# Transposing the softmax A by DMA from the fifth batch on, with a new start and new orders of work in a one-core attention and MLP kernel

## The chip, the cores and the metric

The kernel runs on one core of a Trainium2 chip. A core has TensorE (PE: matmuls and transposes, its weight loads are shown apart as PEld), VectorE (DVE), ScalarE (ACT), GpSimd (POOL), SyncE (SP, which here only issues DMAs) and 16 DMA engines that move data between the core's memory and HBM, or within the core's memory. The engines run beside each other and wait for each other through semaphores. The metric is the time of one execution in microseconds (us): 263.59 before, the median of 15 runs that lie between 263.0 and 264.41.

## The reference

The input is a batch of 8 with 8 heads, 576 tokens and a head size of 64. Attention in the manner of Nyström with 32 landmarks is followed by a two-layer MLP:

```python
q_lm = q.reshape(B, H, m, S // m, D).mean(axis=3)      # m = 32 landmarks of 18 tokens each
k_lm = k.reshape(B, H, m, S // m, D).mean(axis=3)
A  = softmax(scale * q    @ k_lm.T)                    # 576 x 32 for each head
Bm = softmax(scale * q_lm @ k_lm.T)                    # 32 x 32
C  = softmax(scale * q_lm @ k.T)                       # 32 x 576
Z  = Bm.T / (norm1(Bm) * norminf(Bm) + 1e-6)
for _ in range(6):
    Z = 2 * Z - Z @ Bm @ Z                             # Newton steps to the inverse of Bm
x = (A @ Z @ C @ v), heads side by side                # 4608 x 512
h = x @ w_in                                           # w_in 512 x 2048
out = (max(h, 0) ** 2) @ w_out                         # w_out 2048 x 512
```

## The kernel before

Work goes batch by batch. For each batch the attention part makes a transposed softmax A (tile `AT`, heads and landmarks on the partitions, tokens along the row) and a folded weight `G` = Z C v w_in. So the first layer is `h = G^T AT` (`mlp_in`, L822: four matmuls of 288 columns for each of 16 slices of the 2048 features), then ReLU on ACT (L826, tile `r`), the square on DVE (L827, tile `gT`), and the second layer (`mlp_out`, L851: 16 matmuls of 512 columns for each tile of 128 tokens, 36 such tiles in all), whose result is copied out by ACT and stored by ACT's DMA queue.

The attention part of batch b+1 is done while the MLP of batch b runs. Its steps have two-letter names. `pk`, `pq` copy k and q into the layout that is needed (`prepare`, L281), `mk`, `mq` make the segment means on PE with the 0/1 masks `seg` (L342), `tk`, `tq`, `tt` transpose k, q and the last 64 tokens, `lm` and `ls` make the landmark softmax, `ib`, `if`, `jo`, `jl`, `nu`, `nn` are the Newton steps, `sq`, `sk`, `tl` the scores of A and C with their exponentials, `as` the sums of A's rows, `ar` the scaled A (tile `an`, L584, written by DVE), `at` the transpose of `an` into `AT`, `cv` the product of C and v, `wt` and `gg` the folded weight `G`.

In `at` (`a_transposed`, L589 to L598) half a batch, five blocks of 128 tokens by 128, is turned by five PE transposes into PSUM (L596), and copied to `AT` by DVE or ACT (L685). The threshold `DMA_A` says from which batch on a transposing DMA on SP's queue does it instead; at 9 no batch does. The same exists for k and q (`DMA_T` = 3: from the fourth batch on the turning of k, q and their tails goes through SP's queue, L286 and L287).

The order on each of PE, DVE, ACT and SP is written out by hand. `HEAD` orders the first batch's attention (tokens such as `w:16`, 16 filler matmuls of 512 columns whose result nobody reads, or `w:1:256`, one of 256 columns). `PLANS` has one string for each batch: `h` is one slice of `mlp_in`, `s` its square, a bare number is so many matmuls of `mlp_out`, and a step's name does that step for the next batch (with `+` for the batch after). Each engine runs its instructions in the order in which these strings emit them. POOL's queue issues nearly all loads, which turn f32 into bf16 on the way, in one chain (from L132, `load`); `LOADS` is the order of the first of them.

Batch 0's start: SP loads the first k as f32 in one DMA of 1024 KB, and DVE and ACT turn its two halves into bf16 (`ck`, L717 and L718). POOL meanwhile issues the tails of k and q and q in two halves, makes the masks (`seg`, the identity, `mask4`), and then issues the rest of the loads.

Of the kernel before, what the change touches and what calls it, by code (L numbers as in the profile page):

```python
# [9 lines left out]
P = 128  # L10
# [4 lines left out]
BF16 = mybir.dt.bfloat16  # L15
F32 = mybir.dt.float32

B = 8
H = 8
S = 576  # L20
D = 64
M = 32
SEG = S // M
# [4 lines left out]
NC4 = 4  # L28
TAIL = S - NC4 * P
# [3 lines left out]
DMA_A = 9  # L33
# [3 lines left out]
    "w:16 ck tk1 mk w:1:256 w:1:256 ek1d w:1:256 w:1 tk0 tt w:1 w:1 cq0 cq1 ek0a mq tq0 tq1 "  # L37
    "lm w:1 et w:1:256 w:1 eq0a w:1:256 tl eq1d ls sum:0:4:5 w:1 ib w:1 w:1:256 sq1 w:1:256 "
    "if sk1 sum:1:2:5 w:1:256 w:1 sum:1:0:2 jo w:1:256 w:1:256 rec:1 w:1:256 row:1:0:3 "
    "row:1:3:5 w:1:256 sk0 w:1 sq0 jo w:1:256 w:1:256 w:1 w:1:256 sum:0:2:4 sum:0:0:2 w:1 jo "  # L40
    "rec:0 cv:0 cv:1 w:1:256 w:1:256 row:0:3:5 cr jo w:1:256 row:0:0:3 w:1:256 at:1 cba w:1 "
    "jl at:0 ea0d ea1a ct w:1:256 nu w:1:256 g:0 gl1d fv w:1 gf1d w:1 gf0a az gl0d"
)
LOADS = "w10 v0 w00 q1 w01 w11 o0 o1 o2 o3 v1"
PLANS = [
    (
        "pk h g:1 tt h pq h s tk1 s h s h tq1 s tk0 h h mk s s mq tq0 h lm s g:2 g:3 ls sk0 s h "
        "h ib 1 h 1 s if tl h jo 1 sq0 s 1 jo s s 1 h jo 1 sq1 1 jl h 1 nu h s s h nn 2 sk1 nu s "
        "1 s 8 as0 1 ar0 as1 2 ar1 5 nn1 cv 4 wt at0 2 gg0 2 at1 2 gg1 1"
    ),  # L50
    (
        "2 pk 1 h h 1 mk pq s mq 1 s h tq0 lm h ls h tt tq1 3 tl 1 s 1 h ib 1 s if s sq1 2 s h "
        "jo 1 as1 sq0 1 h h s 1 as0 tk1 1 jo 1 s 4 tk0 2 jo 1 h 1 s h 1 pk+ 1 jl ar1 h sk0 1 s 1 "
        "s nu h s 1 sk1 s h h nn s cv nu h 3 nn1 at1 s 3 s wt 3 ar0 2 gg0 3 at0 1 gg1 pq+"
    ),
    (
        "5 mk h 1 h mq s 2 h 5 lm s 2 ls 1 sk1 2 ib 3 h h s sk0 s if 1 s h 2 h 1 jo s h tl 3 jo "
        "1 s 2 h jo 1 s 2 h 3 s sq0 s 1 jl pk+ 4 sq1 2 as0 nu 3 h 1 nn 2 as1 1 pq+ 1 nu 1 h 1 "
        "ar1 h 1 s s h 1 nn1 cv 1 h 2 ar0 1 s wt h 1 at0 2 gg1 1 s at1 1 s 2 gg0 1 s"
    ),  # L60
    (
        "mk 2 h 1 mq 7 h 2 s lm s 1 ls 1 h sq1 1 h h 1 ib 1 s if sk1 1 s h s 2 h jo 1 s 1 h s 1 "
        "jo 2 h 1 pk+ jo 1 tl s h 2 jl as1 sq0 1 s h 1 s h nu s 1 h sk0 s 1 ar1 4 as0 nn 1 ar0 2 "
        "h 3 cv 2 s h nu 4 s nn1 1 at1 1 h wt 2 s 3 s gg1 1 at0 4 gg0 4 pq+"
    ),
    (
        "2 mk h 2 mq 4 h lm 1 h 1 s ls 1 sk0 s ib s 3 h h if 3 tl s 2 h h s 1 s jo 2 h h 1 jo s "
        "1 sq0 s 2 h 1 jo 5 s 10 jl pk+ s 3 sq1 h nu 1 h 1 h 3 as0 sk1 s 1 h 1 as1 ar1 5 s nn cv "
        "nu pq+ 4 s 2 nn1 ar0 h s 4 wt h 2 at0 s 1 gg0 2 s 1 at1 1 gg1 2"
    ),  # L70
    (
        "3 mk mq 3 h lm 3 h h ls 1 s 1 s ib 2 sq1 h 2 if 1 sq0 3 jo h 1 sk0 s jo 2 s h jo tl 4 "
        "as1 1 h 1 jl s sk1 h 3 pk+ s 4 nu h 1 s 2 s 1 s 4 as0 h 1 ar1 nn s 2 ar0 h cv h nu h s "
        "1 s 1 nn1 h 2 h pq+ s wt h 2 at1 2 gg0 at0 5 s 3 s s gg1"
    ),
    (
        "mk 1 mq 3 h s lm 1 h 3 ls 2 h s 1 ib 2 h 1 if sq1 s h 1 s 3 sq0 2 s h 2 s 2 jo h tl 3 "
        "jo 1 h h as0 jo 3 s h 1 s jl 1 s sk1 4 nu 2 as1 h nn 1 h 1 sk0 2 ar0 nu 1 s s 3 h h 1 "
        "cv 2 nn1 s h s 1 at0 1 wt h 2 s 1 ar1 gg0 1 at1 2 s 1 gg1 4 s"
    ),  # L80
    (
        "h 7 h 6 s 1 h 6 h 1 s 2 h s 2 h 6 s 13 h 2 s 2 h 1 s 1 s 5 s h 3 h 1 s s h 11 s 1 h s 8 "
        "h 1 h 1 h 1 s 4 s h 2 s s"
# [5 lines left out]
def kernel(  # L89
# [9 lines left out]
    nc = tc.nc  # L99
# [30 lines left out]
    behind, gate = [], []  # L130

    def load(dst, src, queue=nc.gpsimd):  # L132
        with tc.issue_after(behind[0].ins) if behind else nullcontext():
            d = queue.dma_start(dst, src)  # L134
        if gate:
            tc.add_manual_dep(
                d.ins, gate.pop().ins.name,
                mybir.DependencyInfo(mybir.DependencyClass.Sync, mybir.DependencyReason.DATA),
                reason="q first")
        if queue is nc.gpsimd:  # L140
            behind[:] = [d]
        return d

    def k_row(b):
        return TAIL if b % 2 == 0 else 0

    def q_row(b):
        return TAIL - k_row(b)
# [4 lines left out]
    def staged(b, nm):  # L153
        if (b, nm) == (0, "k"):
            t = stage[:, 0:2 * SIZE].bitcast(F32)
        else:
            o = SIZE * (1 + 2 * b + (nm == "q"))
            t = stage[:, o:o + SIZE]
        return t.rearrange("p (h c d) -> p h c d", h=H, c=NC4)

    def load_qk(b: int, X: dict):

        X["qkt"] = loads.tile([P, H, D], BF16, tag="qkt", name="qkt")

        def tails():
            for src, r0 in ((k, k_row(b)), (q, q_row(b))):
                load(X["qkt"][r0:r0 + TAIL, :, :],
                     src[b, :, NC4 * P:S, :].rearrange("h p d -> p h d"))

        if b > 0:  # L170
            tails()
        for nm, src in (("k", k), ("q", q)):
            if b < 3:
                X[nm + "raw"] = staged(b, nm)
            else:
                X[nm + "raw"] = loads.tile([P, H, NC4, D], BF16, tag="raw", name="raw")
            parts = ((0, H // 2), (H // 2, H)) if b == 0 and nm == "q" else ((0, H),)
            for lo, hi in parts:
                one = load(
                    X[nm + "raw"][:, lo:hi, :, :],  # L180
                    src[b, lo:hi, 0:NC4 * P, :].rearrange("h (p c) d -> p h c d", c=NC4),
                    nc.sync if b == 0 and nm == "k" else nc.gpsimd)
                if b > 0 and nm + "turn" in loaded[b - 1]:
                    tc.add_manual_dep(
                        one.ins, loaded[b - 1][nm + "turn"].ins.name,
                        mybir.DependencyInfo(mybir.DependencyClass.Sync,
                                             mybir.DependencyReason.DATA),
                        reason="behind the turning of the batch before")
            if b == 0 and nm == "k":
                tails()  # L190
# [12 lines left out]
    load_qk(0, loaded[0])  # L203

    def band(t, pattern, base, mult):
        return nc.gpsimd.affine_select(out=t, in_=t, pattern=pattern, compare_op=ALU.is_ge,
                                       fill=0.0, base=base, channel_multiplier=mult)
# [4 lines left out]
    band(seg[:, 0:NC4, :], [[1, NC4], [-SEG, M]], 0, NC4)  # L212
    band(seg[:, 0:NC4, :], [[-1, NC4], [SEG, M]], SEG - 1, -NC4)
    for s, t0 in ((NC4, NC4 * P), (NC4 + 1, NC4 * P - TAIL)):
        band(seg[:, s, :], [[-SEG, M]], t0, 1)
        band(seg[:, s, :], [[SEG, M]], SEG - 1 - t0, -1)
    ident_bf = const.tile([P, P], BF16, name="ident_bf")
    make_identity(nc, ident_bf[:])
    mask4 = const.tile([P, 4], F32, name="mask4")
    nc.vector.memset(mask4[:], 1.0)  # L220
    band(mask4[:], [[-32, 4]], 0, 1)
    masked = band(mask4[:], [[32, 4]], 31, -1)
    blk = const.tile([P, 4, M], F32, name="blk")
    nc.vector.tensor_copy(blk[:], mask4[:, :].unsqueeze(2).to_broadcast([P, 4, M]))
    blk_bf = const.tile([P, 4, M], BF16, name="blk_bf")
    nc.vector.tensor_copy(blk_bf[:], blk[:])
# [11 lines left out]
    nc.vector.tensor_copy(seg[:, NC4 + 2, :], seg[:, NC4, :])  # L238

    def load_rest(after):  # L240

        def w_in(i, j):
            load(
                w_in_bf[64 * i:64 * i + 64, :, 1024 * j:1024 * j + 1024],
                moe_w_in[256 * i:256 * i + 256, 1024 * j:1024 * j + 1024].rearrange(
                    "(j d) f -> d j f", d=D),
            )

        def w_out(j):
            load(  # L250
                w_out_bf[:, 4 * j:4 * j + 4, :],
                moe_w_out[512 * j:512 * j + 512, :].rearrange("(ft fp) c -> fp ft c", fp=P),
            )

        behind[:] = [masked]
        for x in LOADS.split():
            i = int(x[1])
            if x[0] == "w":
                w_in(i, int(x[2]))
            elif x[0] == "o":  # L260
                w_out(i)
            else:
                (load_v if x[0] == "v" else load_qk)(i, loaded[i])

# [33 lines left out]
    def attention(b: int, R: dict):  # L298
# [410 lines left out]
        def head_step(token):  # L709
# [5 lines left out]
            if name == "ck":  # L715
                raw = natural(0, "k")
                dve(X["k"][:, 0:2], raw[:, 0:2])  # L717
                load_rest(act(X["k"][:, 2:4], raw[:, 2:4]))  # L718
                st["qraw"] = natural(0, "q")
                X["tT"] = attn.tile([P, NPAIR, P], BF16, tag="tT", name="tT")  # L720
            elif name[:2] == "cq":
                lo = slice(4 * i, 4 * i + 4)
                dve(X["q"][:, :, lo, :], st["qraw"][:, :, lo, :])
# [250 lines left out]
```

The softmax here doesn't subtract the row's maximum and nothing guards it: scores larger than these inputs give would overflow.

## Time and profile before

| what | value |
|---|---|
| median of 15 runs | 263.59 us (263.0 to 264.41) |
| the profiled execution: time, span | 263.49 us, 261.8 us |
| PE busy | 251.5 us, 96% of the span |
| DVE, ACT, POOL busy | 176.5, 158.3, 45.2 us |
| the first `h` starts | 23.5 us |
| PE transposes of A (L596) | 80, in 16 sets of five |
| copies of AT from PSUM (L685) | 7 on DVE, 449 ns each; 7 on ACT, 640 ns each |
| transposing DMAs on SP's queue | 10 of k and q (T), 5 of the tails (tT) |
| first k on SP's queue | 1024 KB, landed 5.9 us after issue |

The profile is of one execution. Its span is what the engines show; the execution's time is 1.7 us longer. Busy time of PE is generous, since matmuls are pipelined and overlap. A row of a timeline has the start, the duration, the engine, the line, the operation, what it writes and reads, how often, and in brackets the idle time of the engine before it with what ended that. A row of the chain has the start, the duration and what the end was waiting for at that time.

### The profile page before, as it was taken

The page shows a single profiled execution, that of the slowest core. Times are in us where ns is not written, and L with a number is a line of the kernel's source. Part 1 is how long each engine was busy: PE and PEld are TensorE (multiplying, and loading weights), DVE is VectorE, ACT ScalarE, POOL GpSimd, SP SyncE. Part 2 cuts the span into 40 slices and gives each one's busy share as a digit, 9 for nine tenths or more (in the row PEclk, how much of TensorE's full clock was granted, in tenths as well). Part 3 has the DMA queues.
Part 4 walks back from the last instruction along what each step waited for, and adds up shares of the span by engine and source line. Part 5 has one row for each costly group of instructions (what it writes and reads, how often), then busy time and mean ns, then how long its engine had stood idle before and what let it go on. Part 6 is the DMA issues. An engine that isn't in the chain of part 4 may idle for free.

```text
span 261.8 us, 6949 instructions
## 1 busy us (share of the span) xinstructions
PE 251.5 (96%) x2850; PEld 154.1 (59%) x2894; DVE 176.5 (67%) x488; ACT 158.3 (60%) x278; POOL 45.2 (17%) x70
## 2 busy tenths in 40 slices
PE   7898999999999999999999999999999999999994
PEld 2674765476746655666556565666566655555453
DVE  5798777789985888699757588689776793232000
ACT  1556985478755857687557556775777764364210
POOL 8944234110010502501005010600000000000000
PEclk9999999999999999999999999999999999999999
DMA  8999999999539899995858989799501112112122
GB/s 183 200 194 206 206 206 189 210 212 88 115 41 210 128 168 224 149 171 116 136 107 97 198 162 180 107 198 202 108 16 40 43 43 80 40 43 81 40 80 80
DMA packets 69791, 34.65 MB, mean 132 GB/s; under 512 B 37376, under 2 KB 64256, under 8 KB 69760
## 3 DMA queue, kind: packets, MB, share of 16 engines
q0 software_dynamic: 39808, 17.83, 56.4%
q1 hardware_dynamic: 24704, 7.08, 16.1%
q10 hardware_dynamic: 5248, 9.31, 11.0%
q8 instruction: 22, 0.36, 0.6%
q14 instruction: 9, 0.07, 0.1%
HBM read 36.70 MB, written 9.44 MB: 176 GB/s over the span
## 4 chain that ended last, share of the span: by engine, by line
PE 89%; DVE 4%; DMA 2%; issue 2%; ACT 2%
PE ops L851 24%; PE h L822 24%; PE n L851 21%; PE n L530 3%; PE g L805 3%; DMA stage<-in_k_dram 2%; PE n L414 2%; PE n L342 2%; PE n L596 2%; PE idle L295 1%; PE n L614 1%; PE n L313 1%; DVE gT L827 1%; PE n L629 1%; DVE G L703 1%
## 5 line engine op out<-in xcount | busy, mean ns | idle before, releaser
L826 ACT ACTIVATE r<-h 128x576 bf16<-128x576 f32 x128 | 81.3, 652 | 45.5 <-PE h L822 33.7
L851 PE MATMUL ops<-w_out_bf,gT 128*128 128x512 bf16 (+1 forms) x300 | 76.8, 368 | 0.9 <-issue 0.3
L851 PEld LDWEIGHTS <-gT 128*128 128x128 bf16 x592 | 53.2, 98 | 38.7 <-issue 4.2
L827 DVE TENSOR_TENSOR gT<-r 128x576 bf16<-128x576 bf16 x128 | 54.9, 448 | 27.1 <-ACT r L826 27.0
L822 PE MATMUL h<-AT,G 128*128 128x288 bf16 x448 | 71.0, 286 | 0.2
L851 PE MATMUL n<-w_out_bf,gT 128*128 128x512 bf16 x252 | 69.7, 379 | 1.1 <-issue 0.3
L822 PEld LDWEIGHTS <-G 128*128 128x128 bf16 x512 | 47.7, 97 | 24.2 <-ACT AZ L795 0.7
L703 DVE CAST G<-g 128x1024 bf16<-128x1024 f32 x14 | 17.1, 1224 | 5.4 <-PE g L805 5.4
L862 ACT COPY o_sb<-ops 128x512 f32<-128x512 f32 (+1 forms) x19 | 10.9, 574 | 14.5 <-PE ops L851 14.5
L862 ACT COPY o_sb<-n 128x512 f32<-128x512 f32 x17 | 10.0, 587 | 12.9 <-PE n L851 12.8
L703 ACT CAST G<-g 128x1024 bf16<-128x1024 f32 x14 | 14.2, 1014 | 4.5 <-PE g L805 4.5
L295 PE MATMUL idle<-bd 128*128 128x512 bf16 (+1 forms) x47 | 12.3, 384 | 1.6 <-DVE bd L117 1.5
L530 PEld LDWEIGHTS <-T 128*128 128x128 bf16 x256 | 11.3, 98 | 4.2 <-issue 0.6
L134 POOL DMA_DIRECT2D raw<-in_k_dram x5 | 4.5, 890 | 53.0 <-DVE WT L698 15.5
L572 DVE TENSOR_REDUCE ra<-EA 128x20 f32<-128x640 f32 (+3 forms) x19 | 13.2, 703 | 0.3 <-ACT EA L560 0.3
L584 DVE TENSOR_TENSOR an<-EA,rra 128x640 bf16<-128x640 f32 (+2 forms) x18 | 13.2, 736 | 0.2
L530 PE MATMUL n<-bd,T 128*128 128x64 bf16 x256 | 12.7, 193 | 0.3 <-issue 0.2
L535 ACT ACTIVATE EA<-n 128x512 f32<-128x512 f32 x16 | 9.6, 598 | 3.3 <-PE n L530 3.2
L535 ACT ACTIVATE EC<-n 128x512 bf16<-128x512 f32 x16 | 9.5, 596 | 3.0 <-PE n L530 1.6
L134 POOL DMA_DIRECT2D raw<-in_q_dram x5 | 4.4, 885 | 37.2 <-DVE rc L445 17.1
L822 PE MATMUL h<-AZ,G 128*128 128x288 bf16 x64 | 10.0, 286 | 0.6 <-DVE AZ L795 0.4
L414 PEld LDWEIGHTS <-ED 128*128 128x128 bf16 x72 | 6.8, 98 | 6.1 <-DVE EY L453 0.5
(144 smaller groups left out, 286.9 us busy)
## 6 DMA issues: line engine op xcount, KB each, us to landing
out_dram<-o_sb ACTq DMA_DIRECT2D x31, 256.0 KB, 2.9
vm<-in_v_dram POOLq DMA_DIRECT2D x8, 512.0 KB, 10.7
raw<-in_k_dram POOLq DMA_DIRECT2D x5, 512.0 KB, 6.4
raw<-in_q_dram POOLq DMA_DIRECT2D x5, 512.0 KB, 6.1
w_in_bf<-in_moe_w_in_dram POOLq DMA_DIRECT2D x4, 512.0 KB, 11.9
w_out_bf<-in_moe_w_out_dram POOLq DMA_DIRECT2D x4, 512.0 KB, 16.8
out_dram<-o_sb ACTq DMA_DIRECT2D x9, 128.0 KB, 2.4
stage<-in_k_dram SPq DMA_DIRECT2D x1, 1024.0 KB, 5.9
```

The costliest lines, as they stand in the source:

```text
L295: nc.tensor.matmul(idle[:, 0:width], lhsT=z[:, 0:P], rhs=z[:, 0:width], start=True, stop=True)
L414: nc.tensor.matmul(res[a:a + w, qd, :], lhsT=diagonal[a:a + w, qd, :], rhs=moving(qd)[a:a + w], start=True, stop=True)
L530: nc.tensor.matmul(sc[:, c, j, :, :], lhsT=X[nm + "T"][:, c, p, :], rhs=BD[:, 1 if nm == "q" else 0, p, 0:64], start=True, stop=True)
L535: nc.scalar.activation(dst, sc.rearrange("p c j i m -> p c (j i m)"), AF.Exp, scale=SCALE)
L572: nc.vector.reduce_sum(ra[:, quads, lo:hi, :], EA[:, quads, lo:hi, :].rearrange("p q c (h m) -> p q c h m", m=M), axis=AX.X)
L584: on.tensor_tensor(an[:, i, lo:hi, :].rearrange("p c (h m) -> p c h m", m=M), EA[:, i, lo:hi, :].rearrange("p c (h m) -> p c h m", m=M), r ...
L703: (act, dve)[n % 2](G[:, :, n * 512:n * 512 + 512], gg[:])
L822: nc.tensor.matmul(h[:, j, 0:HALF], lhsT=G[:, qd, f * P:(f + 1) * P], rhs=AT[:, qd, a0 + j * HALF:a0 + (j + 1) * HALF], start=(qd == 0), s ...
L826: nc.scalar.activation(r.rearrange("p (j t) -> p j t", j=2), h[:, :, 0:HALF], AF.Relu)
L827: return lambda: nc.vector.tensor_tensor(gT[:, f, o:o + S], r[:], r[:], ALU.mult)
L851: nc.tensor.matmul(ops, lhsT=gT[:, f, t * P:t * P + P], rhs=w_out_bf[:, f, i * n:i * n + n], start=(f == 0), stop=(f == NF - 1))
L862: nc.scalar.copy(o_h, ops)
```

## The change

Three things change together. `DMA_A` goes from 9 to 4, so that for the fifth to the eighth batch (4 to 7) the two halves of `an` are each turned by one transposing DMA on SP's queue, without PE, PSUM and the copies. The first k is loaded in two halves by heads: the first four heads as f32 on SP's queue, the others as bf16 at the head of POOL's queue; the tails, the identity and q follow it there, and the other masks are made only after the first load of v has been issued. The copies that spread the masks on DVE become a step `sm` of `HEAD`. And `HEAD`, `LOADS` and all of `PLANS` are written anew: the fillers go from 51 to 21, batch 0's plan has 12 matmuls of the second layer where it had 36, the loads of w_in and v are in another order.

```diff
-DMA_A = 9
+DMA_A = 4
 HEAD = (
-    "w:16 ck tk1 mk w:1:256 w:1:256 ek1d w:1:256 w:1 tk0 tt w:1 w:1 cq0 cq1 ek0a mq tq0 tq1 "
...
+    "w:8 ck ch1 tk1 tk0 ek0a w:1 ek1d w:1:256 cq0 w:1 mk cq1 w:1 sm tt mq et tq0 eq0a tq1 lm "
...
-LOADS = "w10 v0 w00 q1 w01 w11 o0 o1 o2 o3 v1"
+LOADS = "v0 w10 w00 q1 w11 w01 o0 o1 v1 o2 o3"
 PLANS = [
     (
...
+        "pk h tt h g:1 s pq s tk1 h h tk0 tq1 h mk s s mq h s tq0 lm h h ls ib if sk0 s g:2 s jo "
+        "g:3 tl h jo 2 sq0 s jo h s 1 as0 jl sq1 h h 1 ar0 nu sk1 s s h nn 1 h as1 1 s nu cv nn1 "
+        "h s h wt 2 ar1 at0 gg1 s 1 s s 1 at1 2 gg0"
...
+        "3 mk mq 6 lm 1 ls 2 ib 1 h s h sq0 2 h 3 if sq1 h 1 s s 2 jo h s pk+ 2 sk1 jo 1 h s 1 h "
+        "s tl jo 4 s h 1 as0 h 1 ar0 4 jl 1 s sk0 h 1 h nu as1 s 4 h 2 s nn 2 at0 s 1 h nu ar1 3 "
+        "s h cv nn1 s h s 1 at1 h 2 wt 1 s s 1 pq+ 3 gg0 7 gg1 3"
...
+        "mk h 1 s 7 mq h 1 h lm 2 h 1 sk1 4 s 2 ls ib if 3 s tl 1 s h 1 jo s h 1 s 1 sk0 jo 1 h "
+        "1 cv h s 2 h 2 jo 1 sq0 1 h 2 as0 2 s 1 jl h s s h 1 ar0 s nu 4 sq1 h h 1 as1 4 nn 1 "
+        "ar1 3 s nu 3 h 1 nn1 s 5 s s wt h 4 gg1 at1 s 5 gg0 at0 2"
...
+        "6 h 1 s 6 h 1 h s s 5 h 3 h 1 h s s 1 h s 2 h 4 s 3 h 2 h 1 s 1 s 3 h 2 h s 1 h 1 s 1 s "
...
+    klo = stage[:, 0:SIZE].bitcast(F32).rearrange("p (h c d) -> p h c d", h=H // 2, c=NC4)
...
+    def load_first(X):
+        X["qkt"] = loads.tile([P, H, D], BF16, tag="qkt", name="qkt")
+        X["kraw"], X["qraw"] = staged(0, "k"), staged(0, "q")
+        load(klo, tokens_of(k, 0, 0, H // 2), nc.sync)
+        load(X["kraw"][:, H // 2:H, :, :], tokens_of(k, 0, H // 2, H))
+        for src, r0 in ((k, k_row(0)), (q, q_row(0))):
+            load(X["qkt"][r0:r0 + TAIL, :, :],
+                 src[0, :, NC4 * P:S, :].rearrange("h p d -> p h d"))
+        with tc.issue_after(behind[0].ins):
+            make_identity(nc, ident_bf[:])
+        for lo, hi in ((0, H // 2), (H // 2, H)):
+            load(X["qraw"][:, lo:hi, :, :], tokens_of(q, 0, lo, hi))
...
+    def masks():
+        with tc.issue_after(behind[0].ins):
+            band(seg[:, 0:NC4, :], [[1, NC4], [-SEG, M]], 0, NC4)
...
+            behind[:] = [band(mask4[:], [[32, 4]], 31, -1)]
+
+    def spread_masks():
+        nc.vector.tensor_copy(blk[:], mask4[:, :].unsqueeze(2).to_broadcast([P, 4, M]))
+        nc.vector.tensor_copy(blk_bf[:], blk[:])
+        nc.vector.tensor_copy(seg[:, NC4 + 2, :], seg[:, NC4, :])
...
-                raw = natural(0, "k")
-                dve(X["k"][:, 0:2], raw[:, 0:2])
-                load_rest(act(X["k"][:, 2:4], raw[:, 2:4]))
-                st["qraw"] = natural(0, "q")
+                kraw = natural(0, "k")
+                first_k = klo.rearrange("p h c d -> p c h d")
+                dve(X["k"][:, 0:2, 0:H // 2], first_k[:, 0:2])
+                act(X["k"][:, 2:4, 0:H // 2], first_k[:, 2:4])
+                load_rest()
+                st["kraw"], st["qraw"] = kraw, natural(0, "q")
...
+            elif name == "sm":
+                spread_masks()
+            elif name[:2] in ("ch", "cq"):
+                nm = "k" if name[1] == "h" else "q"
                 lo = slice(4 * i, 4 * i + 4)
-                dve(X["q"][:, :, lo, :], st["qraw"][:, :, lo, :])
+                dve(X[nm][:, :, lo, :], st[nm + "raw"][:, :, lo, :])
```

In the new order SP's queue has, for each of the batches 4 to 7, the two DMAs of A in one run, before, between or behind the transposing DMAs of the next batch's k and q.

## The prediction

> **What bounds the kernel now.** I read the page's busy times first, then the chain that ended last, then a table of stretches cut at the first `h` of each batch, then the chain and the timelines inside the stretches that the change touches. From the page:
>
> ```profile
> PE 251.5 (96%) x2850; PEld 154.1 (59%) x2894; DVE 176.5 (67%) x488; ACT 158.3 (60%) x278; POOL 45.2 (17%) x70
> PE 89%; DVE 4%; DMA 2%; issue 2%; ACT 2%
> ```
>
> PE is the bound, and nine tenths of the chain are matmuls. But this is an average. The stretches (us, busy time and instructions of PE, PEld, DVE, ACT, POOL, clock, DMA share, GB/s):
>
> ```profile
> 0.00:24.00 24.00, 20.88 (x320) 12.94 (x324) 17.84 (x59) 10.73 (x21) 16.33 (x33) 1.00 1.26 194
> 24.00:52.50 28.50, 27.45 (x404) 16.97 (x408) 22.11 (x56) 20.69 (x37) 8.51 (x11) 1.00 1.38 203
> 52.50:78.80 26.30, 25.93 (x349) 17.67 (x353) 23.59 (x65) 19.05 (x33) 2.27 (x3) 1.00 0.93 114
> 190.00:216.00 26.00, 25.46 (x283) 15.68 (x286) 19.41 (x57) 17.86 (x32) 0.00 (x0) 1.00 0.10 32
> ```
>
> From 52.5 us on PE is idle for 0.3 to 0.5 us in a stretch of 26: there a matmul taken away is time taken away. The head (0 to 23.5, where the first `h` starts) is different: PE's figure is padded with the fillers of L295 (3.8 us of the chain), and what runs is a chain of latencies. Its beginning, from the chain in order of time:
>
> ```profile
> 0.81 5.91 DMA stage<-in_k_dram
> 6.74 1.05 ACT nat L718
> 7.84 0.62 PE tps L313 x8
> 8.46 0.51 PE n L342 x20
> ...
> 9.32 0.69 DVE T L729
> 10.01 0.93 DVE nat L723 x2
> ...
> 10.99 0.41 PE n L342 x10
> ```
>
> Two arrivals carry it: k (landed at 6.72) and q's second half, whose DVE copy cannot end before about 10.9. After that DVE has hardly a gap: 5.5 us busy of the 6 from 14 to 20.
>
> **The change, part by part.** The profiled execution took 263.49 us (span 261.8 and 1.7 around it); the median is 263.59, so the sum made from the one holds for the other within 0.1. Less than 0.2% (0.53 us) either way cannot be told from no change.
>
> *The transposes of A leave PE.* Batches 4 to 7 lose two sets of five transposes each: 8 sets. What a set holds on PE is read from when the next matmul starts:
>
> ```profile
> 210.76 0.44 PE L596 MATMUL n<-ident_bf,an 128*128 128x128 bf16 x5
> 211.04 0.38 PE L851 MATMUL n<-w_out_bf,gT 128*128 128x512 bf16 x1
> ...
> 213.39 0.45 PE L596 MATMUL n<-ident_bf,an 128*128 128x128 bf16 x5
> 213.68 0.81 PE L851 MATMUL n<-w_out_bf,gT 128*128 128x512 bf16 x3
> ```
>
> 0.28 us, not the 0.44 in which the pipelined five overlap their neighbours: 8 x 0.28 = 2.2 us (bounds 2.1, from L596's 1.6% of the chain over 16 sets, and 3.5, from 0.44). These stretches have no idle PE to swallow it, so I take 2.2. Four copies of AT on ACT (0.64 each) and four on DVE (0.45) go too; ACT and DVE are idle a quarter of these stretches, so I count 0. If that cover were gone, 4.4 us of engine time would show.
>
> *Eight transposing DMAs on SP's queue, and a wait on PE.* The first `h` of batches 4 to 7 now waits for both. Behind it on PE stands everything, so a late landing is paid in full. The DMA was not run on `an` before. The nearest rows are the same instruction on four blocks (`tT`) and on sixteen (`T`); A has five. Issue to landing, tT and then T:
>
> ```profile
> DMA to landing us min/median/max: 4.3/4.8/6.0
> DMA to landing us min/median/max: 4.4/5.8/8.1
> ```
>
> SP held each tT for 1.3 us, so the pair is landed 1.3 + 4.8 = 6.1 us after the first can issue (bounds 5.5 and 9.6; I take 6.1, since five blocks are nearest to four). The least room is batch 7's. From `ar1` to its first `h` the new order has 29 steps of the output product (0.216 each, from 16 in 3.45 us), two `h` (0.49) and two `gg` (0.56): 8.4 us, 8.7 with the small products. `ar1` takes 0.8 on DVE and may stand behind two squares (0.8): 7.1 us remain, 1.0 to spare. Batch 6 waits after its `ar1` for one DMA (4.8) and has 7.3; batches 4 and 5 have 10 or more. Cost 0; at the upper bound 2.5 us in batch 7. On SP nothing urgent stands behind these DMAs: the T transposes of the next batch follow or go ahead, needed a plan later. DVE's next `ar` waits until the DMA has read `an` (one buffer), some 15 us later: hidden.
>
> A page of the Trainium skill speaks against this: "VectorE: DVE Perf Modes", The three transpose paths, gives 1309 ns for a 128x128 block by DMA against 390 by TensorE. By it a pair of ten blocks would take an estimated 13 us, 6 us more than batch 7 has. The trace's T rows (sixteen blocks inside 8.1 us at worst) disagree, and the sum goes by them.
>
> *k in two halves.* SP's f32 half and POOL's bf16 half go side by side; the 64-KB tails, which shared the queues with k, now follow it. Bytes read from HBM stay, so I bound k's landing by 6.7 (no gain) and 5.3 (both halves at the 383 GB/s that the DMAs reached from 4 to 5 us) and take 5.7. But this is hidden, for the masks move: POOL now issues five DMAs of the first batch's k and q, makes the identity, and issues v's two DMAs before it makes `seg`. From 1.31: 0.81 + 0.70 + 0.70 + 0.35 + 1.54 + 0.97 + 0.69 = 7.1, and the selects (1.3 to 1.6) end at 8.4 to 8.7, against 5.8. So `mk` cannot start before 8.4; it started at 8.30. What gains is q: less stands ahead of it, and its first half is copied before, not behind, T's copy. q's second half landed at about 10.0; now between 9.3 and 10.0, I take 9.5, copied by 10.1, `mq` done at 10.4. Three mask copies (1.3 us before, when POOL was busy; 0.5 to 1.3) now stand on DVE ahead of the copy into `bd`, so that starts near 11.0 instead of 11.44. The landmark exponential then stands on ACT behind T's copy (1.01): 11.85 against 12.43. That is 0.6; the shuffled DVE work behind it (8 us in both) I give another 0.2. Head: -0.8 us, bounds 0 (q no sooner, copies at their full 1.3) and -2.0 (k's whole 1.0 and the 1.0 us in which DVE idles).
>
> *Fewer fillers.* 16 warm-up matmuls become 8, and 35 later ones 13. They end at 4.9 instead of 7.2, and PE then idles until k is there. From the weight loads of the warm-up:
>
> ```profile
> 5.34 0.15 PEld L295 LDWEIGHTS <-bd 128*128 128x128 bf16 x1 [0.28 <-issue]
> 5.73 0.96 PEld L295 LDWEIGHTS <-bd 128*128 128x128 bf16 x5 [0.24 <-issue]
> ```
>
> Until 5.7 one came every 0.43 us, afterwards every 0.2: PE doubled its rate 4.2 us after its first matmul, though the granted clock reads 1.00 throughout. The new order gives it 3.4 us of work before a gap. I take 0, since about 2 us later PE is busy again and the head is held by DVE; upper bound +4.3: some 2.3 us of the head's 7 us of PE work at double length on the chain, and 2 us for the first 4 us of dense `h` at half rate.
>
> "TensorE: Matmul & The Clock Gate", Part 1, states a window of 3.4 us of sustained work, free-running, before full rate. Eight matmuls just fill it, but with the wrong phase the head would start slow. By the page as by the row the price is the 4.3 of the last sentences.
>
> *Orders.* From the first `h` to the last matmul, 23.5 to 258.1, the sum of PE's steady rates is about 230 us of 234.6, so 4.8 are stalls, 3.3 of them before 52.5. The new order does 12 output steps in batch 0's plan instead of 36, and loads v of batch 1 before the last two quarters of w_out. DVE needs 22.1 us there whatever the order, PE then 19.6: the stall stays about 3. I count 0, bounds +2.5 and -2.3.
>
> **Sum:** 263.5 - 2.2 - 0.8 = 260.5.
>
> **Rivals.**
> - *The new orders also close stalls.* For it: 35 fillers became 13, so PE is meant to wait less; 4.8 us of stalls are there. Against: DVE's load in the head and in batch 0's plan. Head -1.5, stalls -2.3: 257.5. Chance 0.18.
> - *PE stays at half rate through the head* (the other side). One mechanism: the gap from 4.9 to about 6.3. For it: full rate came 0.8 us after the new warm-up will have ended. Against: fillers are still strewn in. It decides if PE is slow beyond about 12.5, where half rate falls on the landmark chain; at the bound 260.5 + 4.3 = 264.8, slower. Chance 0.13.
> - *A's transposes land late.* 260.5 + 2.5 (batch 7) + 0.5 (another) = 263.5: no change. For it: 1.0 us of spare; against: the DMAs are idle by then (share 0.10 from 190 to 216). Chance 0.09.
> - *Batch 0's plan is held by DVE*, and the 2.5 us saved elsewhere stall there: 263.0, on the edge of faster. Chance 0.12.
>
> The forecast has 0.48. Faster: 0.48 + 0.18 + half of the last rival = 0.72; same: its other half and 0.04 of the late transposes = 0.10; slower: 0.13 and their other 0.05 = 0.18. The range leaves out the ends of the first two rivals: 257.5 to 264.2; the forecast's own is 259.3 to 261.7.
>
> **What would show it.** L596 x40 instead of x80, eight DMA_TRANSPOSE AT<-an landing in 4.3 to 6 us, and no PE idle time named to them at the first `h` of batches 4 to 7. First `h` at 22.7. `mk` at 8.4 or later, held by POOL's selects, with k landed before 6. Fillers and transposes after 6 us at 0.11 us each, if the rate is halved. Stretches of batches 4 to 6 shorter by 0.56 us each for the same work. I am wrong if the first `h` comes later than 23.5, or if PE idles over 1 us ahead of an `h` of batch 4 to 7.

## The result and the profile after

The changed kernel takes 267.82 us (median of 9 runs, 267.01 to 268.73), against 263.59 before (47 runs); the ratio is 1.0156, 95% interval 1.0144 to 1.0169. Forecast were 260.5 us and a range up to 264.2. The profiled execution took 267.15 us (span 265.0), 6.65 more than the forecast. From its page, busy times and the shares of the chain:

```profile
PE 248.5 (94%) x2781; PEld 151.8 (57%) x2824; DVE 175.5 (66%) x484; ACT 156.5 (59%) x275; POOL 46.1 (17%) x71
PE 78%; DMA 10%; POOL 4%; DVE 3%; issue 2%; ACT 1%; SPq 0%; POOLq 0%; ACTq 0%; DVEq 0%
```

PE has 3.0 us less to do (251.5 before), but the chain has DMA at 10% where it had 2%. The stretches, cut at the first `h` of batches 0 and 1 and at round times behind (same columns as before), show where:

```profile
0.00:23.46 23.46, 17.92 (x287) 11.44 (x290) 16.62 (x58) 10.22 (x21) 16.45 (x33) 1.00 1.24 176
23.46:48.00 24.54, 23.25 (x384) 15.44 (x389) 22.30 (x57) 20.38 (x38) 9.33 (x12) 1.00 1.35 202
...
133.00:162.00 29.00, 25.02 (x218) 14.61 (x221) 16.52 (x46) 14.67 (x28) 1.37 (x2) 0.94 0.80 132
162.00:190.00 28.00, 27.63 (x352) 17.14 (x355) 21.59 (x61) 18.84 (x34) 4.89 (x6) 1.00 1.15 158
190.00:216.00 26.00, 25.63 (x316) 15.75 (x310) 18.07 (x54) 16.57 (x30) 0.00 (x0) 1.00 0.27 69
```

In one stretch alone between the head and the end, 133 to 162, PE lacks 4.0 us, and its clock is 0.94 there and 1.00 in the others. The timelines of POOL, of SP's queue and of PE at that place:

```profile
125.53 0.89 POOL L134 DMA_DIRECT2D raw<-in_k_dram  x1 [15.33 <-DVE ED L409]
126.40 0.90 POOL L134 DMA_DIRECT2D raw<-in_q_dram  x1
127.27 0.91 POOL L134 DMA_DIRECT2D vm<-in_v_dram  x1
128.14 0.72 POOL L134 DMA_DIRECT2D vt<-in_v_dram  x1
```

```profile
128.56 3.98 SPq L595 DMA_TRANSPOSE AT<-an  x2
```

```profile
137.53 0.81 PE L860 MATMUL ops<-w_out_bf,gT 128*128 128x512 bf16 x3
138.66 0.41 PE L831 MATMUL h<-AT,G 128*128 128x288 bf16 x2 [0.33 <-DMA AT<-an]
142.33 0.40 PE L831 MATMUL h<-AT,G 128*128 128x288 bf16 x2 [3.26 <-DMA AT<-an]
```

Four loads (1.6 MB in bf16, cast from f32) were issued in the 3 us before the transposes of batch 4's A. The first half of `AT` is there some 10 us after its issue, at 138.6; the second after 12.4, at 142.29. PE stands for 3.6 us (0.33 and 3.26) at the first `h`. The DMAs of the loads, issue to landing, in the same stretch:

```profile
raw<-in_k_dram POOLq DMA_DIRECT2D x1, 512.0 KB, 6.1
raw<-in_q_dram POOLq DMA_DIRECT2D x1, 512.0 KB, 11.2
vm<-in_v_dram POOLq DMA_DIRECT2D x1, 512.0 KB, 15.1
...
vt<-in_v_dram POOLq DMA_DIRECT2D x1, 64.0 KB, 14.4
```

k and q of this bunch land at 131.6 and 137.6, v and its tail at 142.4 and 142.5: the first transpose was done behind k and q, the second only as the loads ran out. It is not the transposes alone: a store of 256 KB, issued by ACT's queue at the same time, took 8.4 us to landing, where the median of all of them is 2.6. Over all eight DMAs of A the landing is

```profile
DMA to landing us min/median/max: 2.6/3.9/12.4
```

and those of batches 5 to 7, with none of POOL's loads beside them, took 2.6 to 4.4. And PE does not go on at its old pace. Stretches of 2 us behind the wait:

```profile
142.00:144.00 2.00, 1.45 (x11) 1.11 (x12) 0.46 (x1) 1.19 (x3) 0.00 (x0) 0.76 0.64 40
144.00:146.00 2.00, 2.00 (x11) 1.10 (x11) 0.46 (x1) 1.17 (x3) 0.00 (x0) 0.50 0.04 8
146.00:148.00 2.00, 2.00 (x18) 1.24 (x16) 0.00 (x0) 1.46 (x3) 0.00 (x0) 0.89 0.35 131
148.00:150.00 2.00, 2.00 (x15) 1.08 (x13) 0.75 (x4) 0.29 (x1) 0.00 (x0) 1.00 0.00 0
```

The granted clock falls to half behind the 3.26 us without work. From the second half of the first `h` (142.33) to the fifth `h` PE takes 6.69 us:

```profile
149.02 0.65 PE L831 MATMUL h<-AT,G 128*128 128x288 bf16 x4
```

The same work takes 5.17 us at a clock of 1.00 (in the run with fillers below), so the half rate costs 1.5 us; the clock columns would give (0.24 + 0.50 + 0.11) x 2 = 1.7. So this place costs 3.6 + 1.5 = 5.1 us. The expectations below were written with 2.2 for the half rate, 5.8 in all; that was too much. Of the 6.65 missing, 0.8 more is the head: the first `h` starts at 23.46, not at 22.7.

Why the loads came in a bunch is read from the two orders. POOL may load raw k and q of batch 6 only when the copies and transposes of batch 5's have let go of the two buffers. Before, the copy of q (`pq+`) stood almost last in batch 3's plan (token 98 of 98), k's load went out at 122.21 and q's, v's at 140.15 to 141.9. From POOL's timeline before:

```profile
122.21 0.89 POOL L134 DMA_DIRECT2D raw<-in_k_dram  x1 [13.18 <-DVE gT L827]
140.15 0.88 POOL L134 DMA_DIRECT2D raw<-in_q_dram  x1 [17.05 <-DVE rc L445]
```

In the new plan `pq+` and `pk+` are tokens 26 and 34 of 97. The last of their transposes on SP's queue was issued at 119.23 and landed 5.7 us later, at 124.9, and at 125.53 POOL issued k, q and v in one run, 3 us ahead of A.

### The profile page after: what moved, and what is told of

Its sections match the earlier page's. It is cut to its first block, busy times and chain, and to the rows that moved or that the text cites. A ratio compares the mean times of both kernels' runs of the same rounds, so it can differ in the third digit from the quotient of the medians.

```text
span 265.0 us, 6831 instructions
## 1 busy us (share of the span) xinstructions
PE 248.5 (94%) x2781; PEld 151.8 (57%) x2824; DVE 175.5 (66%) x484; ACT 156.5 (59%) x275; POOL 46.1 (17%) x71
## 3 DMA queue, kind: packets, MB, share of 16 engines
q10 hardware_dynamic: 5248, 9.31, 10.1%
## 4 chain that ended last, share of the span: by engine, by line
PE 78%; DMA 10%; POOL 4%; DVE 3%; issue 2%; ACT 1%; SPq 0%; POOLq 0%; ACTq 0%; DVEq 0%
PE h L831 23%; PE ops L860 22%; PE n L860 20%; DMA stage<-in_q_dram 6%; DMA AT<-an 5%; PE n L534 3%; PE g L814 2%; PE n L346 2%; PE n L418 1%; POOL stage L134 1%; PE n L618 1%; POOL qkt L134 1%; PE n L633 1%; PE n L317 1%; DVE gT L836 1%
## 5 line engine op out<-in xcount | busy, mean ns | idle before, releaser
L860 PE MATMUL ops<-w_out_bf,gT 128*128 128x512 bf16 (+1 forms) x300 | 77.9, 368 | 0.9 <-DVE gT L836 0.2
L831 PE MATMUL h<-AT,G 128*128 128x288 bf16 x448 | 72.6, 288 | 3.8 <-DMA AT<-an 3.6
L860 PE MATMUL n<-w_out_bf,gT 128*128 128x512 bf16 x252 | 67.8, 381 | 1.3 <-issue 0.6
L576 DVE TENSOR_REDUCE ra<-EA 128x20 f32<-128x640 f32 (+3 forms) x19 | 13.3, 699 | 0.6 <-ACT EA L539 0.6
L346 PEld LDWEIGHTS <-nat 128*128 128x128 bf16 x256 | 8.5, 98 | 2.6 <-issue 0.8
L134 POOL DMA_DIRECT2D qkt<-in_k_dram x8 | 5.6, 701 | 24.4 <-PE n L356 15.1
L317 PEld LDWEIGHTS <-nat 128*128 128x128 bf16 x96 | 6.9, 110 | 4.9 <-DVE nat L732 2.5
```

The source lines that it names most:

```text
L346: nc.tensor.matmul(means[:, ti, p, :], lhsT=src.rearrange("p h d -> p (h d)"), rhs=seg[:, c + (ti if c == NC4 else 0), :], start=(n == 0 a ...
L576: nc.vector.reduce_sum(ra[:, quads, lo:hi, :], EA[:, quads, lo:hi, :].rearrange("p q c (h m) -> p q c h m", m=M), axis=AX.X)
L831: nc.tensor.matmul(h[:, j, 0:HALF], lhsT=G[:, qd, f * P:(f + 1) * P], rhs=AT[:, qd, a0 + j * HALF:a0 + (j + 1) * HALF], start=(qd == 0), s ...
L860: nc.tensor.matmul(ops, lhsT=gT[:, f, t * P:t * P + P], rhs=w_out_bf[:, f, i * n:i * n + n], start=(f == 0), stop=(f == NF - 1))
```

## The experiments

Two theories for the loss at this place. *Loads*: a transposing DMA is fast alone and slow when casting loads stand ahead of it in the DMA engines. *Transposes*: the five-block DMA, or two in a row on one queue, is that slow at this place whatever else runs.

**Five batches on PE.** Only batches 5 to 7 go by DMA.

```diff
-DMA_A = 4
+DMA_A = 5
```

> The changed kernel with DMA_A = 5: batch 4 turns A by PE again, batches 5 to 7 by DMA. Theory 'loads': the changed kernel loses its time at one place, where the second DMA of batch 4's A, issued at 129.9 us behind four loads of POOL (125.5 to 128.9), landed 12.4 us later. PE stood for 0.3 + 3.3 us and then ran about 4.5 us at half rate (granted clock 0.76, 0.50, 0.89), which is 2.2 more. Then this kernel saves 3.6 + 2.2 and pays two sets of transposes, 0.56: 267.8 - 5.8 + 0.6 = 262.6, and the granted clock is 1.000 again. Rival 'orders': the new orders lose all over the run and the wait is only where it shows: 266 or more.

Measured: 262.21 us (261.84 to 262.3), ratio 0.995 (0.9934 to 0.9967), 5.6 us below the changed kernel although PE has ten transposes more. No PE wait for `AT`; landings 2.6, 3.7 and 4.5 us (least, median, most). The loss is batch 4's alone.

**The load behind the transposes** (the ordered kernel, below). All of the change, but the load of k of batch b+2 is ordered behind the transposing DMA of batch b's A (and with it all that stands behind k on POOL's queue).

```diff
             one = load(X[nm + "raw"][:], tokens_of(src, b))
+            if nm == "k" and b >= 2 and "aturn" in loaded[b - 2]:
+                tc.add_manual_dep(one.ins, loaded[b - 2]["aturn"].ins.name, ...)
...
-                nc.sync.dma_start_transpose(AT[:, i, :]...
+                X["aturn"] = nc.sync.dma_start_transpose(AT[:, i, :]...
```

> The changed kernel, with all eight DMAs of A, but the load of k (and, as POOL issues in order, of q and v behind it) of the batch after next waits until A is turned. Theory 'loads': the transposing DMA is slow only because the loads stand in the same DMA rings ahead of it. Then batch 4's two DMAs land within 3 to 5 us, PE does not wait, and the loads, some 8 us later, are still in time: 267.8 - 5.8 = 262.0. Rival 'transposes': turning 10 blocks takes 10 us and more of itself, or two such DMAs hold each other up; then it still lands about 10 us after issue and the time stays at 267 to 268.

Measured: 261.8 us (261.44 to 262.19), ratio 0.9938 (0.9923 to 0.9953). POOL's timeline and the landings of A:

```profile
134.52 0.89 POOL L134 DMA_DIRECT2D raw<-in_k_dram  x1 [24.59 <-DMA AT<-an]
```

```profile
DMA to landing us min/median/max: 2.6/4.1/5.2
```

The same DMAs at the same time (128.29) land in at most 5.2 us when the loads go out at 134.52, 9 us later, PE does not wait for them, and the time falls by 6.0. This is the cause of the loss, shown by one rule of order. (In the two profiled executions the difference is 5.7: the 5.1 of this place and 0.5 by which the first `h` came earlier, at 22.93.) Whether it is the casting or only the bytes of the loads that hold the transposes up, no run separates.

**The old kernel with A by DMA.** Before, and `DMA_A` = 4 alone.

```diff
-DMA_A = 9
+DMA_A = 4
```

> The kernel before with DMA_A = 4 and nothing else: part one of the change alone. In its old orders the load of k for batch 6 is issued at 122.2 and landed at 128.4, and q and v come at 140.2, so no burst stands ahead of batch 4's A. Theory 'loads': the DMAs land in 3 to 6 us, PE saves 8 x 0.28 = 2.2: 261.4; batch 7, whose second DMA can issue at 213.3 for an h at 216, may give back 0 to 2 of it. Rival 'transposes' (the DMAs take 10 us and more): PE waits at several of the four batches, 266 or more.

Measured: 267.82 us (267.25 to 268.05), ratio 1.0163 (1.0146 to 1.018). I expected 261.4 for the theory that holds, and missed. For batch 4, whose loads are spread here, the DMAs land in 6.5 and 7.1 us and PE does not wait, but batch 5 stalls (and batch 6 for 0.8 us). PE and SP's queue at batch 5:

```profile
166.60 1.14 PE L822 MATMUL h<-AT,G 128*128 128x288 bf16 x4 [3.31 <-DMA AT<-an]
```

```profile
155.70 4.48 SPq L287 DMA_TRANSPOSE T<-nat  x1
160.34 4.47 SPq L591 DMA_TRANSPOSE AT<-an  x2
164.99 1.19 SPq L286 DMA_TRANSPOSE tT<-qkt  x1
```

`an` was ready at 157.23, but a `T` transpose issued at 155.70 held SP's queue for 4.5 us while a load of raw k, issued at 155.13, was under way (one issued at 132.70, with no load beside it, held it for 1.8). The pair for A went out at 160.34 and 162.52, landed in 6.2 and 4.5 us, and `h` had been due at 163.3. So a second door to the same loss: a transposing DMA that is slow because of a load also holds the queue for the next one. The clock was 0.50 from 166 to 172 here. Whether `DMA_A` = 4 gains or loses depends on the order around it; neither this order nor the new one, without the ordered load, leaves it room.

**Is the loss behind the wait the idle time itself?** Twelve fillers are put just ahead of the first `h` of batch 4, inside the wait, into the accumulator that `h` overwrites.

```diff
+        if (b, f) == (4, 0):
+            z = bds[1].rearrange("p a b c -> p (a b c)")
+            for _ in range(6):
+                for j in range(2):
+                    nc.tensor.matmul(h[:, j, :], lhsT=z[:, 0:P], rhs=z[:, 0:512],
+                                     start=True, stop=True)
```

> The changed kernel, still with the late transposes of batch 4, but PE runs twelve filler matmuls of 512 columns (2.6 us at 0.216 each) just ahead of the first h of that batch, inside the wait of about 3.6 us. Theory 'the wait costs twice: 3.6 us idle and then 2.2 us at half rate': PE stays at full rate behind the wait, so 267.8 minus about 2.2, 265.6 (265.2 to 266.2), and the clock in the 4 us behind the wait reads 1.00. Rival 'the slow matmuls behind the wait have another cause': 267.8 or more, and the clock behind the wait reads 0.5 to 0.8 as before.

Measured: 265.99 us (264.84 to 266.29), ratio 1.0091 (1.007 to 1.0112). PE's timeline, and the stretches behind the wait:

```profile
137.84 2.75 PE L831 MATMUL h<-bd 128*128 128x512 bf16 x12
140.43 0.41 PE L837 MATMUL h<-AT,G 128*128 128x288 bf16 x2
142.82 0.41 PE L837 MATMUL h<-AT,G 128*128 128x288 bf16 x2 [1.98 <-DMA AT<-an]
...
147.99 0.65 PE L837 MATMUL h<-AT,G 128*128 128x288 bf16 x4
```

```profile
142.00:144.00 2.00, 1.13 (x11) 0.91 (x12) 0.05 (x1) 0.71 (x2) 0.00 (x0) 1.00 1.41 90
144.00:146.00 2.00, 2.00 (x20) 1.37 (x20) 0.86 (x2) 1.99 (x5) 0.00 (x0) 1.00 0.13 44
```

The transposes are as late as before (12.0 us in the median, 11.2 there), `h` goes on half a microsecond later than in the changed kernel, and yet 1.8 us are won: with a gap of 1.98 us in place of 3.26 the clock stays at 1.00. From the second half of the first `h` to the fifth it is 5.17 us (142.82 to 147.99) in place of 6.69: the half rate had cost 1.5 us, and useless work made the kernel faster. The medians differ by more than the profiled executions (266.01 against 267.15, 1.0 of it behind this place); what the rest of the 1.8 is stays open. "TensorE: Matmul & The Clock Gate" of the Trainium skill, HAM oscillation, speaks of gaps beyond some 3.4 us that put PE back to half rate. The trace agrees about the size (3.26 and 3.31, a little less than that, were enough; 1.98 was not).

**What are the start and the orders worth without A by DMA?**

```diff
-DMA_A = 4
+DMA_A = 9
```

> The changed kernel with DMA_A back at 9: new start, new orders and loads, all of A's transposes on PE. Theory 'the start and the orders are worth almost nothing, the transposes 2.2': the ordered kernel (261.8) plus the 2.2 us of eight sets on PE, 264.0 (263.4 to 264.6). Rival 'the orders carry the gain': near 262, as low as the kernel with five batches on PE (262.2). PE has no wait for AT before an h of batches 4 to 7 in either.

Measured: 264.16 us (11 runs, 263.24 to 264.94), ratio 1.0036 (1.0023 to 1.0048). Against the ordered kernel this is 2.4 us more by medians (2.6 by the ratios): the 2.2 for eight sets of transposes held. But start and orders together cost 0.4% where I forecast a gain.

**The short warm-up**, in the changed kernel and in the ordered one:

```diff
-    "w:8 ck ch1 tk1 tk0 ek0a ...
+    "w:16 ck ch1 tk1 tk0 ek0a ...
```

> The changed kernel with 16 warm-up matmuls in place of 8. In the changed kernel's head a filler of 512 columns still takes 0.43 us at 9.3 to 10.4, and the segment means of k start at 10.38 where POOL's masks were there at 8.8: PE runs at half rate until about 13.5. Theory 'cold': with the gap filled PE is at full rate from about 5.7, the means start at 9.0 to 9.4, and the first h about 1.0 us earlier than 23.46: 266.8. Rival 'DVE': the head is held by DVE and by the arrival of q whatever PE's rate: the first h stays within 0.3 us of 23.46 and the time at 267.8.

> The changed kernel with the load of k put behind A's transposes, and 16 warm-up matmuls in place of 8. Theory 'the short warm-up leaves PE at half rate': the first h comes near 22.7 in place of 22.9 to 23.5, and the time is 0.5 to 0.9 below 261.8, so about 261.1. Rival 'the head is held by q and DVE': no change, 261.6 to 262.0.

Measured: 266.94 us (266.13 to 269.46), ratio 1.0149 (1.0098 to 1.02), for the first; its first `h` is at 22.67 with `mk` at 8.81. For the second, 261.74 (261.12 to 262.98), ratio 0.9942 (0.9923 to 0.9961), first `h` 22.81: no change from 261.8. The profile of the changed kernel does show the half rate:

```profile
5.24 0.40 PE L317 MATMUL tps<-ident_bf,nat 128*128 128x128 bf16 x2
7.84 1.68 PE L317 MATMUL tps<-ident_bf,nat 128*128 128x128 bf16 x14 [2.21 <-DVE nat L732]
9.31 1.27 PE L299 MATMUL idle<-bd 128*128 128x512 bf16 x3
10.38 0.64 PE L346 MATMUL n<-seg,nat 128*128 128x32 bf16 x16
```

Three fillers take 1.27 us (0.43 apart; 0.70 with `w:16`), and `mk` starts at 10.38. But with the same eight warm-up matmuls the first `h` came at 23.46, 22.93, 22.87, 22.89 and 22.50 in five profiles of different kernels: the size of this loss changes from one execution to the next. That slow matmuls explain the 0.6 to 0.8 us by which the profiled execution's first `h` trails the two kernels with `w:16` is likely and not shown: of the five profiles the one with the first `h` at 22.50 has slow matmuls until 12.7 too (a filler of 512 columns takes 0.59 there at 9.77). On the median the runs could not resolve it.

**k's second half as f32 through SP's queue**, on top of the last one.

```diff
-        load(X["kraw"][:, H // 2:H, :, :], tokens_of(k, 0, H // 2, H))
+        load(khi, tokens_of(k, 0, H // 2, H), nc.sync)
```

Here `khi` is a place for f32 in the staging area, from which the copy `ch1` then reads.

> As the kernel with 16 warm-up matmuls and the ordered load, but the second half of the first k also goes as f32 through SP's queue, and POOL's queue begins with the tails. Theory 'the casting half of k lands late and delays q behind it': k's second half lands by 6.2 in place of 7.1, q's second half by 10.0 in place of 10.7, and the time falls by about 0.5, to 260.6. Rival 'the masks hold mk and DVE holds the rest': both land sooner and the first h comes within 0.2 of where it was, no change.

Measured: 260.12 us (259.37 to 261.0), ratio 0.988 (0.9861 to 0.9898): 1.6 us below the kernel it is built on, three times what I expected, and the lowest median of all that ran. DVE's timelines, first with k's second half through POOL, then through SP:

```profile
6.77 0.66 DVE L739 COPY nat<-stage 128x1024 bf16<-128x1024 bf16 x1 [1.48 <-DMA stage<-in_k_dram]
...
10.46 0.56 DVE L739 COPY nat<-stage 128x1024 bf16<-128x1024 bf16 x1 [0.65 <-DMA stage<-in_q_dram]
```

```profile
6.52 0.77 DVE L741 CAST nat<-stage 128x1024 bf16<-128x1024 f32 x1 [1.38 <-DMA stage<-in_k_dram]
...
9.83 0.43 DVE L741 COPY nat<-stage 128x1024 bf16<-128x1024 bf16 x1 [0.17 <-DMA stage<-in_q_dram]
```

k lands 0.25 sooner (6.5), q's second half 0.6 sooner, POOL has one DMA less to issue. The first `h` moves from 22.81 to 21.92, 0.9. The other 0.7 is behind it: in the chain of both kernels the piece after the head is a DMA, the raw q of batch 1.

```profile
12.31 15.00 DMA stage<-in_q_dram
27.34 0.70 DVE nat L291
```

```profile
12.07 13.47 DMA stage<-in_q_dram
25.57 0.70 DVE nat L293
```

**The old start with the new plans** (A by DMA, the load ordered): `HEAD`, the loads of the first k and q and the masks as before the change, w_in's first quarter ahead of v.

```diff
-LOADS = "v0 w10 w00 q1 w11 w01 o0 o1 v1 o2 o3"
+LOADS = "w10 v0 w00 q1 w11 w01 o0 o1 v1 o2 o3"
...
-    "w:8 ck ch1 tk1 tk0 ek0a ...
+    "w:16 ck tk1 mk w:1:256 w:1:256 ...
```

> The start and HEAD of the kernel before, with the changed kernel's plans, A's transposes from batch 4 on by DMA and the load of k ordered behind them. Theory 'the new start is worth 0 to 0.6': 261.8 to 262.4. If the new start had brought the forecast's 0.8: 262.6. If it costs: below 261.8.

Measured: 261.39 us (260.62 to 261.94), ratio 0.9922 (0.9907 to 0.9937). Its first `h` is at 23.54, 0.6 later than in the ordered kernel, and its time is 0.4 lower (the intervals overlap). A head that is 0.6 us shorter was worth nothing there.

**Is it q of batch 1?** In the best kernel one load of w_in is issued ahead of k and q of batch 1 in place of behind them.

```diff
-LOADS = "v0 w10 w00 q1 w11 w01 o0 o1 v1 o2 o3"
+LOADS = "v0 w10 w00 w11 q1 w01 o0 o1 v1 o2 o3"
```

> The kernel with both halves of k on SP's queue, 16 warm-up matmuls and the ordered load (260.1, first h 21.9, q of batch 1 landed 25.6), with one load of 512 KB of w_in issued before k and q of batch 1 in place of behind them. Theory 'behind the first h the next bound is the landing of q of batch 1': the first h stays at 21.9, q lands 1 to 2 us later and the time rises by as much, to 261.1 to 262.1. Rival 'the first h alone sets the gain of that kernel': the first h and the time stay, 259.8 to 260.5.

Measured: 262.01 us (11 runs, 261.51 to 263.25), ratio 0.9954 (0.994 to 0.9968), 1.9 more. The first `h` is at 22.05, as good as unmoved; DVE's copies of batch 1's k and q, and the PE that waits:

```profile
24.95 0.69 DVE L293 COPY nat<-stage 128x2048 bf16<-128x2048 bf16 x1 [2.21 <-DMA stage<-in_k_dram]
27.60 0.69 DVE L293 COPY nat<-stage 128x2048 bf16<-128x2048 bf16 x1 [0.60 <-DMA stage<-in_q_dram]
```

```profile
26.03 0.61 PE L325 MATMUL n<-ident_bf,nat 128*128 128x128 bf16 x8 [2.17 <-DVE tT L677]
```

q's copy is 2.0 later, k's 2.4 (it started at 22.54), and the time 1.9 up. PE's wait ends with the copy of `tT`, which stands behind k's copy on DVE, so PE meets the late k first. Behind the head the arrival of batch 1's k and q sets the pace; which of the two, this run does not separate.

**One batch more by DMA**, in the best kernel, A of batch 3 too, both DMAs where the first stood.

```diff
-DMA_A = 4
+DMA_A = 3
...
-        "cv nn 6 nu 3 at0 h 1 nn1 1 h s 4 wt 6 gg1 s 4 at1 s gg0 5"
+        "cv nn 6 nu 3 at0 at1 h 1 nn1 1 h s 4 wt 6 gg1 s 4 s gg0 5"
```

> The kernel with both halves of k on SP's queue, 16 warm-up matmuls and the ordered load (260.1), with one batch more by DMA: A of batch 3 too, both its transposes issued where the first stood, the load of k two batches on ordered behind them. Theory 'each batch moved is worth 0.55 us once its transposes find nothing ahead of them': 259.6 (259.3 to 259.8) and no PE wait for AT at the first h of batch 3. Rival 'batch 3 meets T's transposes on SP's queue, as batch 5 did with the orders of before': PE waits 1 us or more there, and the time is 260.6 or more.

Measured: 260.19 us (259.62 to 261.46), ratio 0.9887 (0.9864 to 0.991). Neither theory is met: no wait for `AT` (landings up to 6.7), and no gain. In the profiled executions it was 0.42 us late by 73 us, where both kernels still do the same, and only 0.10 late by 105, past the plan in which batch 3's A is made, so that plan gave back 0.3. A step of this size is lost in the scatter of six runs; what the batch is worth stays open.

## Why the prediction was wrong, point by point

- **The transposes leave PE: -2.2.** Held: L596's 80 became 40 (now L600), and the ordered kernel lies 2.4 to 2.6 below the one with all of A on PE.
- **"Eight transposing DMAs on SP's queue, and a wait on PE ... Cost 0."** This step failed: it cost 3.6 us of wait and, behind it, 1.5 at half rate. The sign that I had named (PE idle for over 1 us ahead of an `h` of batch 4 to 7) was there, with 3.26. I took the pair's landing as 6.1 us from the first issue, with 9.6 as the upper bound; in batch 4 it was 13.7 (1.3 + 12.4). I called batch 7 the least room; it was the DMAs' quietest place (2.6). Batch 4 had 9.8 us (128.56 to 138.33), as I had reckoned, but the landings of `T` and `tT` that I took as price had no such bunch of loads ahead of them: the loads of raw k and q wait for those very transposes. I looked at what stands behind the new DMAs on SP's queue, and never asked what the moved `pq+` releases on POOL's. The rival "A's transposes land late" was right that a late landing holds PE, at the wrong batch, without the cause, and with 3.0 us for what cost 5.1.
- **The figure of the Trainium skill, "VectorE: DVE Perf Modes", The three transpose paths.** The estimate of 13 us by it for the pair comes close to batch 4's 13.7, but for no good reason: by 1309 ns a block every DMA of five would take 6.5, and six of the eight took 4.4 or less. The row that I set against it was right about the instruction, and wrong about the queue.
- **A price that no term had: PE at half rate behind a stall, 1.5.** I priced the gate in the head alone (+4.3 at most) and a late landing by its idle time alone. The filler run shows that the idle time has this second bill.
- **The head: -0.8.** The first `h` gained 0.07 in the profiled execution, and 0.6 to 1.0 in four others with the same start. k's half through POOL landed at 7.1, where I took 5.7 for both; q's second half at 10.7, where I took 9.5: a 256-KB half that is cast on the way took 5.8 us, and q stands behind it. `mk` was not held by POOL's selects (ready at 8.8) but by PE, at 10.38.
- **Fewer fillers: 0.** The half rate was there until about 13.5 us, as the rival said it might be, but its cost is far from 4.3, and not to be seen on the median (261.8 with 8, 261.74 with 16 in the ordered kernel).
- **Orders: 0, and the head's gain kept in full.** Start and orders together came out at +0.4% of the time, about +0.9 us, against -0.8. The chain before has no load of batch 1 in it (k and q copied at 24.1 and 25.6). In the new order POOL issues q 0.9 later, and its copy starts at 27.05, 1.4 later, in the chain. What the head wins is given back there: this was the stall that is late next, and I did not look for it. The later issue is not the cause, though: with the old start POOL issues q at 11.52, as before (11.51), and with the new plans and loads it lands 15.3 us later in place of 13.3. What there makes it late, and what the rest of the 0.9 is, no run shows.

The sum with measured terms: 263.6 + 0.9 (start and orders) - 2.4 (transposes) + 3.6 (wait) + 1.5 (half rate) = 267.2; measured 267.8, so 0.6 is not placed (in the profiled execution the head, 0.5 later than in the ordered kernel, is most of it).

## What to carry to other kernels

Before a copy is handed to the DMA engines, look on every queue at what is issued just ahead of it (here 1.6 MB in the 3 us before), after the reordering and not before: a prefetch that is early for no one can be ordered behind it (here that was worth 6.0 us). A stall of PE can have a second bill in the clock; where it cannot be avoided, filler matmuls inside it are worth a try (here 1.8 us). And when a head is shortened, name the arrival that comes next, since it may have moved the other way.

## What the runs showed of the hardware that was not expected

- One transposing DMA of five blocks landed in 2.6 to 5.2 us in the ordered kernel, with the loads out of its way, and in 10.1 and 12.4 us behind 1.6 MB of casting loads; the second landed only as these ran out.
- At its issue such a DMA held SP's queue for 1.2 to 2.7 us, and one of sixteen blocks, with a load under way, for 4.5 us; the next one started only then.
- A PE gap of 3.26 us brought the granted clock to 0.76, 0.50 and 0.89 in the next three stretches of 2 us (1.5 us lost), one of 3.31 us kept it at 0.50 from 166 to 172 us, one of 1.98 us did nothing to it.
- 512 KB as f32 landed in 3.7 us by SP's queue; 256 KB of bf16, cast from 512 KB of f32, in 5.8 us by POOL's; they were issued at 0.8 and 1.3 us.
